# Phi loaded into the place of its transposed softmax, and the softmax's step ahead of the last mixing step

## The chip, the cores and the metric

The kernel runs on one core of a Trainium2 chip. The metric is the device time of one execution in microseconds (us), the median of several runs. The core has TensorE (PE in the profile; PEld is its weight load), VectorE (DVE), ScalarE (ACT), GpSimd (POOL) and SyncE (SP), whose queue issues the DMAs.

## The reference

For each of 8 batches and 8 heads with 576 tokens, head dimension 64 and 32 memory slots:

```python
a = exp(phi - max(phi, axis=2)); a = a / (sum(a, axis=2) + 1e-9)   # over the 576 tokens
k_m = einsum('bhsm,bhsd->bhmd', a, k)
v_m = einsum('bhsm,bhsd->bhmd', a, v)
attn = softmax(q @ k_m.T / 8)                                      # over the 32 slots
x = (attn @ v_m)  reshaped to [8, 576, 512]
u = x + real(fft(fft(x, axis=1), axis=2))
un = (u - mean(u)) / sqrt(var(u) + 1e-6)
out = u + relu(un @ w_ch1) @ w_ch2                                 # 512 -> 2048 -> 512
```

## The kernel before

There are two strands of work. **The feed-forward part (FFN)** runs over 18 chunks of 256 tokens. A chunk has 8 weight slices; for each slice `ffn1` makes 24 matmuls of 256 columns into `ph`, ScalarE and VectorE split the result into two 16-bit parts in `hring`, and `ffn2` makes 12 matmuls of 512 columns into `po`. Matmuls in 16 bits come in threes (high by high, high by low, low by high).

**The background** is a generator that makes the tokens `u` that the FFN takes, one batch after the other; a batch gives 4.5 tiles of 128 tokens, 2.25 chunks. Its steps for a batch are:

- the softmax of Phi over the tokens (`pooling_weights`): Phi (four DMAs of 160 KB, one for each pair of heads, `load_phi`) is transposed in 20 matmuls into three PSUM banks (`pl` and two `pf`, of a pool of four called `psg`), VectorE takes maxima (L398, L403), ScalarE the exponentials (L409, L410) into `pht`, VectorE the sums and reciprocals; then for each half ScalarE and VectorE write the high and the low part into `elt` (L418, L419), and a DMA transpose writes them into `et` (L301);
- for four pairs of heads: load the pair's k, v and q (`load_pair`; even pairs into `rawt`, odd pairs into `stg[:, 0]`, 640 KB for k and v and 384 KB for q), squares on ScalarE (L526, L529) that one matmul sums over the partitions (`pm<-scratch,small`), scaling and splitting (L541 to L547), the products with `et` (`pm<-et,stg`), and one step later the scores (`psc`) and their softmax. The transposed scores go into `stacks` by DMA transposes; stacks 0 and 1 lie in `attnT`, stacks 2 and 3 in `phs`;
- `values` (the transform of v_m over features, `pv`, and a DMA transpose into `vbdt`), `spectrum` (the transform over tokens, `pa` into `at`);
- three mixing steps: `mix_m` (`pp_t`), `mix_x` (`px_t`, which reads the stacks) and `add_mix` (L835) write `u` into a ring of 8 tiles. A mixing step waits in the program until the ring has room.

Between two `yield`s lies one step. After each weight slice but a chunk's last the loop takes at most one step, and at a chunk's end as many as the chunk after next needs. Batches 0 and 1 are special: they run at the start beside the loading of the weights, and batch 1's softmax is made apart by `next_weights`.

Before the change `phs` is the place of Phi, its first part `pht` the place of the exponentials, and its whole later that of stacks 2 and 3. `et` has 2560 16-bit elements for each partition, as many bytes as `phs`. In batches 2 to 7 the softmax is the batch's first step, and its loads stand at its head:

```python
        if b:
            load_phi(b)
        pl = psg.tile([P, 512], F32, tag="g", name=f"pl_{b}")
```

The order of each engine's queue and of SP's DMAs isn't the program's: a scheduler that works the timeline out ahead fixes it at build time, with the program's order as priority, so that a load can stand far ahead of its step when its place is free. Each engine then runs its own queue strictly in order.

Of the kernel before, what the change touches and what calls it, by code (L numbers as in the profile page):

```python
# [10 lines left out]
F32 = mybir.dt.float32  # L11
# [10 lines left out]
B, H, S, D, M = 8, 8, 576, 64, 32  # L22
NG = H // 2
# [5 lines left out]
NST = 5  # L29
KV = NST * 2 * P  # L30
KVP = KV + NST * 2 * M
# [10 lines left out]
NX = 2  # L42
# [95 lines left out]
def kernel(  # L138
# [10 lines left out]
    nc = tc.nc  # L149
# [11 lines left out]
    phs = const.tile([P, NST, NG, 2 * M], F32, name="phs")  # L161
    pht = phs.rearrange("p t g c -> p (t g c)")[:, : 2 * S].rearrange("p (g s) -> p g s", g=2)
    elt = const.tile([P, 2, NST * P], F16, name="elt")
    et = const.tile([P, 2, 2, NST, P], F16, name="et")
# [21 lines left out]
    identf = const.tile([P, P], F32, name="identf")  # L186
# [6 lines left out]
    stg = const.tile([P, 3, 4 * UW], F16, name="stg")  # L193
# [15 lines left out]
    def of_kind(t, w):  # L209
        return t[:, :, 1:3] if w else t[:, :, 0::3]  # L210

    qs = [stg[:, 2, 2 * nk + i * NQ : 2 * nk + (i + 1) * NQ] for i in range(2)]
    et32 = et.rearrange("p g l t c -> p (g l t c)").bitcast(F32).rearrange("p (g t c) -> p g t c", g=2, t=NST)


# [36 lines left out]
    def tiny(tag, n, bufs=2):  # L252
        if tag not in rings:
            rings[tag] = [taken[0], 0]
            taken[0] += n * bufs
        o, i = rings[tag]
        rings[tag][1] += 1
        o += i % bufs * n
        assert taken[0] <= 464, taken
        return scratch[:, o : o + n]  # L260
# [62 lines left out]


    def load_phi(b):
        for g in range(NG):
            nc.sync.dma_start(out=phs[:, :, g], in_=raw[b, g, :, KV:KVP].rearrange("p (t c) -> p t c", t=NST))

    def load_pair(b, g):
        r = rawt  # L330
# [53 lines left out]

    def pooling_weights(b):

        if b:
            load_phi(b)
        pl = psg.tile([P, 512], F32, tag="g", name=f"pl_{b}")
        mx = tiny("mx", 4, 2)  # L390
        pf = []
        for g in range(2):
            pf.append(psg.tile([P, 512], F32, tag="g", name=f"pf_{b}_{g}"))
            for t in range(NST):
                dst = pf[g][:, t * P : (t + 1) * P] if t < 4 else pl[:, g * P : (g + 1) * P]
                marks["pe"] = nc.tensor.transpose(dst, phs[:, t, 2 * g : 2 * g + 2].rearrange("p g c -> p (g c)"), identf)
            if b >= NX:
                nc.vector.tensor_reduce(out=mx[:, g : g + 1], in_=pf[g], axis=AX.X, op=ALU.max)  # L398
        rest = pl[:, : 2 * P].rearrange("p (g s) -> p g s", g=2)[:, :, : S - 4 * P]
        if b < NX:  # L400
            pooling_f32(b, pl, pf, rest)
            return
        nc.vector.tensor_reduce(out=mx[:, 2:4], in_=rest, axis=AX.X, op=ALU.max)  # L403
        nc.vector.tensor_tensor(out=mx[:, 0:2], in0=mx[:, 0:2], in1=mx[:, 2:4], op=ALU.max)
        nc.vector.tensor_scalar(out=mx[:, 0:2], in0=mx[:, 0:2], scalar1=-1.0, scalar2=None, op0=ALU.mult)
        su = tiny("su", 4, 2)
        for g in range(2):
            m = mx[:, g : g + 1]
            nc.scalar.activation(pht[:, g, : 4 * P], pf[g], AF.Exp, bias=m, accum_out=su[:, g : g + 1])  # L409
            nc.scalar.activation(pht[:, g, 4 * P :], rest[:, g], AF.Exp, bias=m, accum_out=su[:, 2 + g : 3 + g])  # L410
        nc.vector.tensor_tensor(out=su[:, 0:2], in0=su[:, 0:2], in1=su[:, 2:4], op=ALU.add)
        nc.vector.tensor_scalar(
            out=su[:, 0:2], in0=su[:, 0:2], scalar1=1e-9, scalar2=2.0**-EB, op0=ALU.add, op1=ALU.mult
        )
        nc.vector.reciprocal(out=su[:, 2:4], in_=su[:, 0:2])
        for g in range(2):
            r = su[:, 2 + g : 3 + g]
            nc.scalar.activation(elt[:, 0, :S], pht[:, g], AF.Copy, scale=r)  # L418
            nc.vector.scalar_tensor_tensor(  # L419
                out=elt[:, 1, :S], in0=pht[:, g], scalar=r, in1=elt[:, 0, :S], op0=ALU.mult, op1=ALU.subtract  # L420
            )
            transpose(
                et[:, g].rearrange("p l t c -> p (l t) c"), elt.rearrange("p l c -> p (l c)"), False, f"et_{b}_{g}"
            )
# [241 lines left out]
    def pair_transpose(b, g, ahl, attnT):  # L666
        if b:
            transpose(stacks[g], ahl.rearrange("p t k m -> p (t k m)"), False, f"attnT_{b}_{g}")
        else:
            transpose(attnT[:, g], ahl.rearrange("p t c -> p (t c)"), True, f"attnT_{b}_{g}")  # L670
# [497 lines left out]
    marks = {}  # L1168
# [6 lines left out]
    def background():  # L1175

        nt = 0
        u2, half_made = None, None
        for b in range(B):
            n = f"{b}"  # L1180
            ivs = tiny("ivs", NG)
            mem, ahl = {}, {}
            if b != 1:
                pooling_weights(b)
            yield (nt if half_made is None else half_made), 0
            if b == 0:

                for g in range(NG + 1):
                    if g < NG:
                        km = memory_f32(b, g, first[g], vmf, [0])  # L1190
                        mem[g] = first[g][:, KV:], None, km, 1.0 / 8.0
                    if g > 0:
                        ahl[g - 1] = pair_scores(b, g - 1, *mem.pop(g - 1), aeo)
                for g in range(NG):
                    memory_f32(b, g, first[g], vmf, [1])
            for step in range(NG + 2) if b > 0 else ():
                if step < NG:
                    r = load_pair(b, step)
                if step >= 2:
                    pair_transpose(b, step - 2, ahl.pop(step - 2), attnT)  # L1200
                if 0 <= step - 1 < NG:
                    ahl[step - 1] = pair_scores(b, step - 1, *mem.pop(step - 1), aeo)
                    yield (nt if half_made is None else half_made), 0
                if step < NG:
                    mem[step] = pair_memory(b, step, r, vmf, ivs)
                    yield (nt if half_made is None else half_made), 0
            vbd, vh, isg, igx, isq = values(b, vmf, ivs, ahl)
            yield (nt if half_made is None else half_made), 0
            at = spectrum(b, aeo)
            if b == 0:  # L1210
                transpose(vbdt, vbd, True, f"vbd_{b}")
                vbd = vbdt.rearrange("p (l g) f -> p l g f", l=2)
            for g in sorted(ahl):
                pair_transpose(b, g, ahl.pop(g), attnT)
            full = slice(0, P)
            for t in (0, 1, 2) if b % 2 == 0 else (2, 0, 1):
                yield (nt if half_made is None else half_made), 2 if t < 2 else 1 - b % 2
                if t == 2:
                    if b % 2 == 0:
                        u2 = uring[:, len(allocs) % NU]  # L1220
                        us[nt] = u2
                        allocs.append(nt)
                        half_made = nt
                        nt += 1
                    rows = slice(64 * (b % 2), 64 * (b % 2) + 64)
                    tm = mix_m(b, "t2", slice(256, 320), rows, at, vh, isg, isq)
                    px = mix_x(b, "t2", 4 * P + 64, 64, rows, attnT, vbd)
                    add_mix(u2, rows, px, igx, tm, 0)
                    half_made = nt - 1 if b % 2 == 0 else None
                    continue  # L1230
                tm = mix_m(b, f"t{t}", slice(t * P, (t + 1) * P), full, at, vh, isg, isg)
                for sign in range(2):
                    c0 = (2 * t + sign) * P
                    px = mix_x(b, f"t{t}{sign}", c0, P, full, attnT, vbd)
                    u = uring[:, len(allocs) % NU]
                    allocs.append(nt)
                    add_mix(u, full, px, igx, tm, sign)
                    us[nt] = u
                    nt += 1
            yield (nt if half_made is None else half_made), 0  # L1240
        while True:
            yield n_tiles, 0

    load_phi(0)
    marks["q"] = nc.sync.dma_start(out=mk, in_=mk_d)
    for g in range(NG):
        with tc.issue_after(marks["q"].ins):
            marks["q"] = nc.sync.dma_start(
                out=phi_next[:, :, g], in_=raw[1, g, :, KV:KVP].rearrange("p (t c) -> p t c", t=NST)
# [37 lines left out]
    for j in range(3):  # L1287
        load_weights(j)

    bg = background()  # L1290
    made, room = 0, 0

# [61 lines left out]
    for n in range(NW, n_steps):  # L1354
        c, j = divmod(n, NW)
# [97 lines left out]
```

## Time and profile before

| | |
|---|---|
| runs shown | 921.36, 923.54, 942.75 us; median 923.54 us |
| profiled execution | 920.78 us, its span 919.0 us |
| TensorE busy | 907.8 us, 99% of the span |
| VectorE, ScalarE, GpSimd busy | 622.3, 493.4, 266.6 us |
| granted TensorE clock | 1.0 |
| DMA queues | 100.16 MB, mean 109 GB/s |

The span runs from the first to the last instruction of the profiled execution; the time includes what lies around it. An engine's idle time is laid to what ended it. Matmuls are pipelined: the time of one (272 ns for 256 columns) is longer than the step from one to the next.

### The profile page before, as it was taken

Reading aid. Unit: us, or ns where it says so; the run is one execution under the profiler, and the core shown is the slowest. Engines: PE = TensorE matmul, PEld = TensorE weight load, DVE = VectorE, ACT = ScalarE, POOL = GpSimd, SP = SyncE. Lnnn points to the kernel's source line nnn. Section 1 sums busy time; section 2 is a strip of 40 time slices with the busy share of each in tenths; the row PEclk is TensorE's granted clock in tenths of the full one; section 3 lists DMA queues with packets and bytes.
Section 4 is the critical chain, followed back from the end, with each engine's and each line's share of the span. In section 5 each row is a group of like instructions: output and inputs, shape, how many; then the busy total and the mean of one; then the engine's idle time right before and its main releaser. Section 6 shows DMA issues by size and latency. Waiting matters only on the chain.

```text
span 919.0 us, 19338 instructions
## 1 busy us (share of the span) xinstructions
PE 907.8 (99%) x7796; PEld 671.4 (73%) x7796; DVE 622.3 (68%) x1471; ACT 493.4 (54%) x955; POOL 266.6 (29%) x302
## 2 busy tenths in 40 slices
PE   9999899999999999999999999999999999999998
PEld 8976567667766766776766667777676767688887
DVE  5979967667578775787554876676666776554554
ACT  4658867645464654664444564665555554533331
POOL 1304524224145231463143441152222231300000
PEclk9999999999999999999999999999999999999999
DMA  9938842433436352545224433365235353210000
GB/s 323 414 146 287 212 90 53 98 84 83 82 76 165 78 125 55 144 84 147 42 69 113 119 80 110 53 138 127 67 77 111 88 149 103 47 47 1 24 14 34
DMA packets 132761, 100.16 MB, mean 109 GB/s; under 512 B 115008, under 2 KB 115264, under 8 KB 130624
## 3 DMA queue, kind: packets, MB, share of 16 engines
q1 hardware_dynamic: 132672, 98.93, 40.9%
q8 instruction: 61, 1.00, 0.5%
q14 instruction: 28, 0.23, 0.1%
HBM read 62.35 MB, written 13.63 MB: 83 GB/s over the span
## 4 chain that ended last, share of the span: by engine, by line
PE 83%; DVE 7%; ACT 4%; issue 2%; DMA 2%; POOL 1%; SPq 0%; POOLq 0%; DVEq 0%; ACTq 0%
PE ph L318 34%; PE po L949 28%; PE po L1011 6%; PE pm L318 2%; PE pp_t L318 2%; PE psc L318 2%; PE po L910 1%; PE pa L748 1%; DMA et<-elt 1%; PE ph L893 1%; PE px_t L318 1%; PE pm L497 1%; DVE w2s L1100 1%; POOL ud L880 1%; PE idle L296 1%
## 5 line engine op out<-in xcount | busy, mean ns | idle before, releaser
L318 PE MATMUL ph<-unring,w1t 128*128 128x256 f16 x3264 | 389.0, 272 | 0.0
L318 PEld LDWEIGHTS <-w1t 128*128 128x128 f16 x3264 | 314.2, 98 | 58.8 <-issue 3.1
L949 PE MATMUL po<-w2s,hring 128*128 128x512 f16 x1344 | 310.1, 379 | 0.0
L949 PEld LDWEIGHTS <-hring 128*128 128x128 f16 x1344 | 130.0, 98 | 132.2
L940 DVE SCALAR_TENSOR_TENSOR hring<-ph,hring 128x512 f16<-128x512 f32 x112 | 76.0, 680 | 28.0 <-ACT hring L939 26.5
L939 ACT ACTIVATE hring<-ph 128x512 f16<-128x512 f32 x112 | 65.8, 589 | 52.0 <-PE ph L318 52.0
L859 POOL TENSOR_TENSOR scratch<-scratch,small 128x1 f32<-128x1 f32 x36 | 24.2, 674 | 180.1 <-DVE scratch L858 154.1
L634 POOL TENSOR_TENSOR aring<-aring,scratch 128x384 f32<-128x384 f32 x28 | 25.4, 908 | 165.5 <-DVE scratch L632 159.7
L880 POOL TENSOR_TENSOR ud<-un,ud 128x1024 f16<-128x1024 f32 x17 | 37.1, 2184 | 34.1 <-ACT ud L879 34.1
L318 PEld LDWEIGHTS <-stg 128*128 128x128 f16 x912 | 35.4, 97 | 6.3 <-issue 2.9
L658 ACT CAST aeo<-eo 128x384 f16<-128x384 f32 x30 | 15.3, 511 | 41.6 <-DVE eo L655 41.6
L628 ACT ACTIVATE aring<-aring,scratch 128x384 f32<-128x384 f32 x24 | 14.6, 610 | 42.4 <-DVE aring L627 42.3
L835 DVE SCALAR_TENSOR_TENSOR uring<-px_t,scratch,share 128x256 f32<-128x256 f32 (+1 forms) x80 | 34.2, 476 | 1.4 <-PE px_t L318 1.4
L646 ACT CAST at<-aring 128x640 f16<-128x640 f32 x28 | 20.3, 724 | 26.3 <-POOL aring L634 26.3
L618 DVE TENSOR_REDUCE scratch<-psc 128x12 f32<-128x384 f32 x32 | 17.5, 548 | 24.6 <-PE pm L318 18.9
L910 PE MATMUL po<-w2s,hring 128*128 128x512 f32 x64 | 31.2, 609 | 2.0 <-ACT hring L896 2.0
L1033 POOL TENSOR_TENSOR uring<-uring,share 128x256 f32<-128x256 f32 x3 | 2.2, 728 | 105.9 <-ACT share L1030 105.9
L821 DVE SCALAR_TENSOR_TENSOR share<-pp_t,scratch,small 128x257 f32<-128x257 f32 (+1 forms) x48 | 21.0, 480 | 15.5 <-ACT small L818 15.3
L651 DVE TENSOR_TENSOR eo<-aring 128x128 f32<-128x128 f32 x29 | 25.7, 885 | 8.5 <-POOL aring L649 8.5
L893 PE MATMUL ph<-unring,w1t 128*128 128x256 f32 x128 | 30.6, 383 | 0.0
L649 POOL TENSOR_TENSOR aring<-aring 128x128 f32<-128x128 f32 x56 | 30.0, 557 | 1.8
L893 PEld LDWEIGHTS ph<-unring,w1t 128*128 128x128 f32 x128 | 23.8, 190 | 7.7 <-issue 5.0
(320 smaller groups left out, 1546.3 us busy)
## 6 DMA issues: line engine op xcount, KB each, us to landing
out<-uring SPq DMA_DIRECT2D x35, 256.0 KB, 2.1
rawt<-in_raw SPq DMA_DIRECT2D x13, 640.0 KB, 5.2
stg<-in_raw SPq DMA_DIRECT2D x13, 640.0 KB, 5.3
stg<-in_w SPq DMA_DIRECT2D x7, 1024.0 KB, 6.8
rawt<-in_raw SPq DMA_DIRECT2D x15, 384.0 KB, 3.2
stg<-in_raw SPq DMA_DIRECT2D x15, 384.0 KB, 3.2
phs<-in_raw SPq DMA_DIRECT2D x28, 160.0 KB, 3.2
w2s<-in_w SPq DMA_DIRECT2D x4, 1024.0 KB, 11.0
```

Of the source, the lines that this page charges most:

```text
L318: m = nc.tensor.matmul(out, lhsT=lhsT, rhs=rhs, start=start, stop=stop)
L634: eng.tensor_tensor(out=a, in0=a, in1=sm.unsqueeze(2).to_broadcast([P, 12, M]), op=ALU.mult)
L649: eng.tensor_tensor(out=a2[:, i : i + 4], in0=a[:, 0:4], in1=a[:, 4:8], op=op)
L651: nc.vector.tensor_tensor(out=eo[:, 1:3, 0], in0=ap[:, 1:3, 0], in1=ap[:, 1:3, 1], op=ALU.add)
L835: nc.vector.scalar_tensor_tensor(out=u[rows, hs], in0=px[rows, hs], scalar=igx[rows], in1=tm[rows, w * NJ + half : w * NJ + half + 256], o ...
L880: marks[f"ul{c}"] = nc.gpsimd.tensor_tensor(out=ud[:, 1], in0=un, in1=ud[:, 0], op=ALU.subtract)
L893: nc.tensor.matmul(ph, lhsT=w[:, k, f * P : (f + 1) * P], rhs=unTs[0][:, k], start=(k == 0), stop=(k == NK - 1))
L910: nc.tensor.matmul(po[t], lhsT=h[:, f, t], rhs=w[:, f], start=(j == 0 and f == 0), stop=(j == NW - 1 and f == UB - 1),)
L939: marks["fa"] = nc.scalar.activation(h[:, 0], phv, AF.Relu)
L940: marks["fd"] = nc.vector.scalar_tensor_tensor(out=h[:, 1], in0=phv, scalar=0.0, in1=h[:, 0], op0=ALU.max, op1=ALU.subtract)
L949: nc.tensor.matmul(po[t], lhsT=hs[j][:, lh, f * 2 + t], rhs=w2s[:, j * UB + f, lw, :], start=(j == 0 and f == 0 and i == 0), stop=(j == NW ...
L1011: m = nc.tensor.matmul(po[n], lhsT=h[:, la, a], rhs=b[lb], start=(j == 0 and i == 0 and n in ("p1", "p6", "p5", "p4")), stop=(j == NW - 1 ...
```

## The change

Three things are done. Phi of batches 2 to 7 is loaded into the bytes of `et` (`phi_own`), where the transposed softmax will lie, and not into `phs`; the load stands after `values` of the batch before. The exponentials go into the first 1152 32-bit elements of `stg[:, 0]` (`pht_own`), where the odd pairs' k and v lie, and not into `phs`. And the softmax's step of batches 3 to 7 stands ahead of the last mixing step of the batch before, that of batch 2 at batch 1's end, where it was.

```diff
+    pht_own = stg[:, 0].bitcast(F32)[:, : 2 * S].rearrange("p (g s) -> p g s", g=2)
+    phi_own = et.rearrange("p g l t c -> p (g l t c)").bitcast(F32).rearrange("p (t g c) -> p t g c", t=NST, g=NG)
...
     def load_phi(b):
+        dst = phi_own if b else phs
         for g in range(NG):
-            nc.sync.dma_start(out=phs[:, :, g], in_=raw[b, g, :, KV:KVP].rearrange("p (t c) -> p t c", t=NST))
+            nc.sync.dma_start(out=dst[:, :, g], in_=raw[b, g, :, KV:KVP].rearrange("p (t c) -> p t c", t=NST))
...
     def pooling_weights(b):
-        if b:
-            load_phi(b)
+        phi, pht = (phi_own, pht_own) if b else (phs, None)
...
-                marks["pe"] = nc.tensor.transpose(dst, phs[:, t, 2 * g : 2 * g + 2].rearrange("p g c -> p (g c)"), identf)
+                marks["pe"] = nc.tensor.transpose(dst, phi[:, t, 2 * g : 2 * g + 2].rearrange("p g c -> p (g c)"), identf)
...
-            if b != 1:
+            if b == 0:
                 pooling_weights(b)
-            yield (nt if half_made is None else half_made), 0
+            if b < NX:
+                yield (nt if half_made is None else half_made), 0
...
             vbd, vh, isg, igx, isq = values(b, vmf, ivs, ahl)
+            if 0 < b < B - 1:
+                load_phi(b + 1)
             yield (nt if half_made is None else half_made), 0
...
-            for t in (0, 1, 2) if b % 2 == 0 else (2, 0, 1):
+            for i, t in enumerate((0, 1, 2) if b % 2 == 0 else (2, 0, 1)):
+                if i == 2 and 1 < b < B - 1:
+                    yield (nt if half_made is None else half_made), 0
+                    pooling_weights(b + 1)
                 yield (nt if half_made is None else half_made), 2 if t < 2 else 1 - b % 2
...
+            if b == 1:
+                yield (nt if half_made is None else half_made), 0
+                pooling_weights(2)
             yield (nt if half_made is None else half_made), 0
```

`NX` is 2.

## Rows read from the trace of the kernel before

**Rows 1.** The page: busy time of the engines, and the granted clock in 40 slices.
```profile
PE 907.8 (99%) x7796; PEld 671.4 (73%) x7796; DVE 622.3 (68%) x1471; ACT 493.4 (54%) x955; POOL 266.6 (29%) x302
...
PEclk9999999999999999999999999999999999999999
```

**Rows 2.** The chain of waits in order of time: start us, us, what.
```profile
175.06 4.08 DMA et<-elt
...
204.25 2.59 PE po L949 x12
...
241.17 2.62 PE ph L318 x24
...
278.00 3.41 DMA et<-elt
...
377.87 3.40 DMA et<-elt
```

**Rows 3.** The waits of TensorE: us in total, times, longest.
```profile
PE pm L318 <- DMA et<-elt: 2.2, 2, 1.9
...
PE pv L721 <- ACT share L702: 1.7, 1, 1.7
```

**Rows 4.** Windows: length, then busy us (instructions) of each engine; clock, DMA, GB/s.
```profile
92.00:140.00 48.00, 44.12 (x294) 30.78 (x293) 38.86 (x99) 35.19 (x65) 18.86 (x22) 1.00 0.60 145
...
240.00:285.00 45.00, 43.06 (x366) 30.32 (x365) 29.61 (x68) 23.59 (x51) 17.16 (x16) 1.00 0.39 87
...
780.00:919.00 139.00, 135.67 (x1185) 114.50 (x1181) 70.98 (x176) 47.11 (x72) 11.34 (x10) 1.00 0.11 28
```

**Rows 5.** Timeline of batch 3's softmax: start us, us, instruction, idle before it.
```profile
258.16 2.10 SPq L327 DMA_DIRECT2D phs<-in_raw  x4
...
265.07 0.60 PE L396 MATMUL pf<-identf,phs 128*128 128x128 f32 x4
...
270.32 0.21 ACT L410 ACTIVATION_READ_ACCUMULATOR phs<-pl,scratch 128x1 f32 x1
...
281.55 0.69 PE L318 MATMUL pm<-et,stg 128*128 128x64 f16 x20 [1.94 <-DMA et<-elt]
...
282.18 0.72 ACT L526 ACTIVATE stg<-stg 128x640 bf16<-128x640 f32 x1
282.31 0.82 DVE L419 SCALAR_TENSOR_TENSOR elt<-phs,scratch,elt 128x576 f16<-128x576 f32 x1 [1.81 <-ACT elt L418]
...
283.62 0.83 ACT L529 ACTIVATE stg<-stg 128x768 bf16<-128x768 f32 x1
```

**Rows 6.** Timeline of batch 3's pair 1: the matmul that sums its squares.
```profile
288.01 0.17 PE L318 MATMUL pm<-scratch,small 128*128 128x3 bf16 x1
```

**Rows 7.** Timelines of batch 2's softmax and its pairs 0 and 1.
```profile
152.71 3.15 SPq L327 DMA_DIRECT2D phs<-in_raw  x4
...
161.24 0.49 PE L396 MATMUL pf<-identf,phs 128*128 128x128 f32 x3
...
179.19 0.69 PE L318 MATMUL pm<-et,stg 128*128 128x64 f16 x20 [0.27 <-DMA et<-elt]
...
180.04 0.82 DVE L419 SCALAR_TENSOR_TENSOR elt<-phs,scratch,elt 128x576 f16<-128x576 f32 x1 [4.19 <-ACT elt L418]
...
185.80 0.17 PE L318 MATMUL pm<-scratch,small 128*128 128x3 bf16 x1
```

**Rows 8.** DMA issues by target and source: count, KB each, median us to landing.
```profile
stg<-in_raw SPq DMA_DIRECT2D x13, 640.0 KB, 5.3
...
phs<-in_raw SPq DMA_DIRECT2D x28, 160.0 KB, 3.2
```

**Rows 9.** The waits of SP's own queue: us in total, times, longest.
```profile
SPq L327 <- PE px_t L318: 52.8, 6, 13.7
```

**Rows 10.** Timeline of SP: loads of pair 1 for batches 2 and 3.
```profile
31.67 0.33 SPq L339 DMA_DIRECT2D stg<-in_raw  x1
...
225.76 2.42 SPq L339 DMA_DIRECT2D stg<-in_raw  x2
```

## The prediction, made before the change was run

> **What bounds the kernel now.** I read the page first. TensorE is busy for 99% of the span at full granted clock throughout, VectorE for 68%, ScalarE for 54% [rows 1]. A busy share alone doesn't prove a bound, so I looked at the pace of matmuls next: in the chain of waits, 24 ffn1 matmuls of 256 columns take 2.62 us (109 ns each) and 12 ffn2 matmuls of 512 columns take 2.59 us (216 ns each), and these two rows repeat with the same figures from 180 us to 890 us [rows 2]. That is one column per cycle at 2.4 GHz with nothing between. So where TensorE shows no gap, it issues at its pace, and only its gaps can be won.
>
> Then its gaps. TensorE's waits [rows 3] hold 2.2 us for the transposed softmax `et`: 1.94 us in batch 3 [rows 5] and 0.27 us in batch 2 [rows 7]; after 130 us no other line of TensorE stands in that list. The windows say the same from the other side: 240 to 285 us has 43.06 of 45.00 us busy, which is the gap of batch 3. What is left lies outside the change's reach or at its edge: 3.9 us idle between 92 and 140 us, of which 1.7 us wait for `share` in batch 1's values, and 3.3 us after 780 us, when all eight batches are mixed [rows 3, 4].
>
> **Part 1, Phi into `et`.** Removed: the four phi loads' wait for the last mixing step, because `phs` also holds stacks 2 and 3. The load's issue waits on SP for `px_t` 52.8 us in six batches [rows 9]; that is a queue's wait, not TensorE's. In batch 3 the loads are issued at 258.16 us, right after the last mixing matmuls, and the first transpose of Phi starts at 265.07 us: 6.9 us [rows 5]; in batch 2 it is 152.71 to 161.24 us: 8.5 us [rows 7]. Landing takes 3.2 us of it [rows 8]; the rest is issue, and a TensorE queue that has other work first. The new loads need only that the batch before has used `et` in its four memory products, tens of us earlier. The bytes are the same, four times 160 KB [rows 8]. The moved issues pass other work on SP, at 2.1 us for four [rows 5]; the DMA that follows them there (the transpose of vbd or an output) has slack, so I cost this at nothing; without that slack it would be 2.1 us in each of six batches, 12.6 us, if all of it came through to TensorE.
>
> **Part 2, exponentials into the raw odd pairs' place.** The exponentials and the two scalings by batch are the same instructions with another address: 0. But pair 1's k and v of the same batch lie there too. Today they are loaded a whole batch ahead: the pair that batch 3 uses at 282.18 us was issued at 225.76 us, and batch 2's already at 31.67 us [rows 5, 10]. After the change this load cannot start before the second `elt` difference has read the exponentials. In batch 3 that ends at 282.31 + 0.82 = 283.13 us [rows 5]. Now the new chain: 5.3 us to landing [rows 8] gives 288.4 us; the three squares run from 282.18 to 283.62 + 0.83 = 284.45 us today [rows 5], 2.3 us, so they would end at 290.7 us. TensorE's one matmul that sums their results stands at 288.01 us [rows 6]. **At the old place of the softmax the new wait would cost 2.7 us**; batch 2 gives the same: 180.86 + 5.3 + 2.3 = 188.5 against 185.80 us [rows 7], 2.7 us. Behind that matmul on TensorE stand ffn1 and ffn2, since its queue is in order, so this would be lost in full. It is covered if the softmax ends at least 2.7 us earlier.
>
> **Part 3, the softmax's step in front of the last mixing step.** I walked through the counters that decide which step is taken with which weight slice. Batch 2's softmax keeps its slot; batches 3 and 7 swap it with the last mixing step and so get it one slot earlier, while pair 0 stays; batches 4, 5 and 6 get the softmax, and pair 0 too, at least one slot earlier (batch 5's softmax a whole chunk). No chunk's normalisation moves. A slot holds 2.62 + 2.59 = 5.2 us of FFN on TensorE [rows 2]. So in batches 3 to 7 the softmax moves forward by about 6.9 us of phi wait and 5.2 us of slot, against 2.7 us needed; in batch 2 by up to 8.5 us. The new load is hidden, and the `et` waits go: -2.2 us. What is late next is nothing that TensorE shows.
>
> The cost that stays unknown is in TensorE's queue order: it is worked out ahead, instruction by instruction, and one wrong guess of a DMA's time gave the 1.94 us gap of batch 3 [rows 5]. The new load of 640 KB is one more such guess in six batches. Lower end: none, and the phi guess that goes instead is worth up to the 2.2 us; upper end: 2.7 us in each batch. I take 0, nearest to the rows in which pair loads today hide, and keep both ends.
>
> A rule that speaks for more: the Trainium skill, "Perfetto Trace Analysis", section "Identifying the Most-Contended Engine", says that matmul busy time is no good measure of how near TensorE is to its limit and names the weight loads' busy share instead. That is 73% here and would leave 27% of the span, some 248 us, as room. The rows disagree: twelve 512-column matmuls fill 2.59 us without a gap [rows 2] and need only one load apiece, so the load path idles while the columns run at full pace.
>
> **The sum** against the profiled execution: 920.78 us (its span is 919.0 us, 1.8 us lies around it) - 2.2 = 918.5 us. The three runs shown have a median of 923.54 and a lowest of 921.36 us, so usual runs stand 0.6 to 2.8 us above the profiled one, the middle 1.7: 918.5 + 1.7 = 920.2. I forecast **920 us**.
>
> **Rivals.**
> (a) *The new wait takes over.* Pair 1's load behind the exponentials comes late to the sum's matmul: 2.7 us in each of six batches, 16 us: 936 us. It decides from the point where a batch's softmax ends less than 2.7 us earlier than now relative to pair 1. Against it: 6.9 us of phi wait gone. For it: in batch 2 nothing else helps, since its softmax keeps its slot. Batch 2 alone gives 923 us; four batches give 931 us.
> (b) *PSUM banks; slower.* The softmax holds three of the four banks of its pool from the first transpose to the last exponential, 265.07 to 270.53 us, 5.5 us [rows 5]. Now the last mixing step, which needs two banks, comes behind it in five batches. If its matmuls stand in TensorE's queue with no FFN between, it costs 5.5 us in each: 27 us, 947 us, 2.6% slower than the median. It decides where less than 5.5 us of FFN lies between; a slot holds 5.2 us, which leaves 0.3 us a batch, and in batches 4, 5 and 6 the mixing waits for the chunk's end anyway.
> (c) *Gain at the start.* Phi of batch 2 no longer waits, so its 20 transposes (0.11 us apart, 2.2 us) and what follows may fill part of the 3.9 us idle before 140 us [rows 4]: 920 - 3.9 = 916 us at best, and 920.78 - 2.2 - 3.9 = 914.7 us if the runs come as low as the profiled one.
> (d) *It does nothing.* The `et` wait in batch 3 comes from the order, not from Phi's arrival, and comes back elsewhere: 922.5 us.
> (e) *TensorE has room.* The chain holds 4.08, 3.41 and 3.40 us of `et` transpose for batches 2, 3 and 4 [rows 2]; if such pieces were time that TensorE could win, 10.9 us came out in place of 2.2: 911.5 us. Against it stands that TensorE shows only 2.2 us of waits in these places [rows 3]. The section of the Trainium skill cited above would lead here.
>
> **How the numbers follow.** The forecast, with anything from -3 to +2 us about it, 0.60; (a) in one to all batches 0.17; (b) 0.05; (c) 0.08; (d) 0.07; (e) 0.03. Two per cent, 18.5 us, is about what a measurement here tells from no change: faster means below 905 us, slower above 942 us. Faster holds only what goes beyond (e), 0.01. Slower holds most of (b) and a doubled (a), where the issue on SP adds its 2.1 us in each batch, 0.05. The rest, 0.94, is within. The range 914 to 932 us takes in (c), (d), and (a) up to four batches with the 0.6 us by which runs scatter; outside stay (a) in all batches, (b) and (e).
>
> **What would show it.** Right: no TensorE wait for `et` in the waits; the phi loads' issue 10 us and more ahead of the transposes in every batch, with no SP wait for `px_t` at that line; pair 1's k and v issued after the second `elt` difference, and the squares of pair 1 still over before the sum's matmul; TensorE full between 140 and 780 us. Wrong: a gap in front of the sum's matmul or pair 1's products (a), a gap in front of `px_t` or `pp_t` with the exponentials as releaser (b), a changed idle sum before 140 us (c). A TensorE that stays full while the time moves by more than 5 us would mean that its pace, not its gaps, had changed, and that I misread the bound.

## The result and the profile after

The changed kernel takes 926.53 us (median of six runs, 925.53 to 945.31), the kernel before 921.65 us in the same session (median of six); the ratio is 1.0055 with a 95% interval of 1.0041 to 1.0068. Forecast was 920 us and a small gain. Runs of both kernels near 943 us show a lower mean clock (0.978 in the changed kernel's) and are left out of every ratio and of the table's medians, and the profile of experiment 10 below is of such a run. The profiled execution took 926.56 us with a span of 924.8 us: 5.8 us more than before.

The page, busy time of the engines (compare [rows 1]): the same 7796 instructions on TensorE, 2.1 us more busy, and 3.7 us more idle.

```profile
PE 909.9 (98%) x7796; PEld 670.1 (72%) x7796; DVE 624.2 (67%) x1471; ACT 493.1 (53%) x955; POOL 267.8 (29%) x302
```

TensorE's waits from 130 us on: total us, times, longest (compare [rows 3]). Both `et` waits are gone. In their place stand five others, 6.2 us in place of 2.2 when added up from the timelines: 4.0 us more.

```profile
PE pm L320 <- ACT stg L528: 2.7, 1, 2.7
PE psc L320 <- DVE scratch L589: 1.6, 1, 1.6
PE psc L320 <- ACT scratch L588: 0.9, 1, 0.9
PE pm L320 <- POOL stg L546: 0.7, 1, 0.7
PE pm L320 <- ACT stg L543: 0.2, 1, 0.2
```

Windows of the same kernel (length, busy us of each engine, then granted clock, DMA share, GB/s). The first three follow the largest wait; the last three answer to [rows 4].

```profile
178.00:183.50 5.50, 2.89 (x40) 2.55 (x38) 1.85 (x7) 1.84 (x7) 0.00 (x0) 1.00 0.73 179
183.50:187.00 3.50, 3.38 (x10) 1.34 (x10) 2.86 (x11) 2.62 (x5) 0.00 (x0) 0.51 0.02 5
187.00:193.00 6.00, 6.00 (x46) 3.95 (x44) 5.18 (x8) 3.37 (x6) 4.84 (x6) 1.00 0.38 95
...
92.00:140.00 48.00, 44.39 (x300) 31.32 (x300) 38.93 (x101) 35.69 (x67) 19.67 (x22) 1.00 0.58 144
240.00:285.00 45.00, 44.27 (x397) 31.61 (x395) 29.43 (x70) 24.27 (x52) 15.78 (x15) 1.00 0.41 100
780.00:925.00 145.00, 141.45 (x1246) 118.87 (x1242) 75.90 (x189) 49.57 (x78) 11.88 (x11) 1.00 0.10 27
```

Right behind the wait the granted clock stands at half (0.51, the 1.2 GHz level) for 3.4 us, which costs 1.7 us. Twelve ffn2 matmuls take 4.30 us there (timeline of batch 2 below); counted the same way they take 2.75 us at full clock, in a timeline of the kernel before:

```profile
187.35 2.75 PE L949 MATMUL po<-w2s,hring 128*128 128x512 f16 x12
```

With 4.0 us of waits that is 5.7 of the 5.8 us. The half clock does not come in every run: two of the changed kernel's runs have a mean clock of 1.000 and take 925.53 and 925.79 us, the profiled one and another 0.998 and 926.5 us, one 0.996 and 928.4 us. It is slower without it too.

**Batch 2**, timeline of the kernel after: start us, us, instruction, idle before it (compare [rows 7, 10]).

```profile
159.09 0.60 PE L398 MATMUL pf<-identf,et 128*128 128x128 f32 x4
...
176.85 0.82 DVE L421 SCALAR_TENSOR_TENSOR elt<-stg,scratch,elt 128x576 f16<-128x576 f32 x1 [3.73 <-ACT elt L420]
...
177.69 0.33 SPq L342 DMA_DIRECT2D stg<-in_raw  x1
...
182.02 0.74 ACT L528 ACTIVATE stg<-stg 128x640 bf16<-128x640 f32 x1 [3.02 <-DMA stg<-in_raw]
...
183.38 0.19 ACT L528 ACTIVATION_READ_ACCUMULATOR stg<-stg 128x1 f32 x1
183.62 0.17 PE L320 MATMUL pm<-scratch,small 128*128 128x3 bf16 x1 [2.73 <-ACT stg L528]
183.81 4.30 PE L951 MATMUL po<-w2s,hring 128*128 128x512 f16 x12
```

Read it from the bottom. TensorE's sum matmul waits for ScalarE's squares, these for pair 1's k and v, and the load that brings them is issued 0.02 us after the second `elt` difference has ended at 177.67 us; before, it was issued at 31.67 us [rows 10]. Phi itself is early: its loads go out at 35.70 us, in the timeline of SP in the kernel after, where they went out at 152.71 us [rows 7].

```profile
35.70 13.16 SPq L330 DMA_DIRECT2D et<-in_raw  x4
```

Still the first Phi transpose comes only 2.15 us earlier than before (159.09 for 161.24 us), and the second `elt` difference 3.2 us (177.67 for 180.86 us). TensorE has no wait in front of these transposes; the order in which it takes its queue sets this, not Phi.

**Batch 4**, timeline of the kernel after: score steps of VectorE beside instructions of GpSimd, and the two waits of `psc`.

```profile
395.09 2.13 POOL L882 TENSOR_TENSOR ud<-un,ud 128x1024 f16<-128x1024 f32 x1
395.16 2.13 DVE L654 SCALAR_TENSOR_TENSOR eo<-aring,small 128x64 f32<-128x64 f32 x1 [0.40 <-POOL aring L636]
...
398.76 2.16 POOL L962 TENSOR_TENSOR un<-w2s 128x1024 f32<-128x1024 f16 x1
398.87 2.27 DVE L657 TENSOR_TENSOR eo<-aring 128x192 f32<-128x192 f32 x1
401.06 0.28 DVE L569 TENSOR_REDUCE scratch<-pm 128x64 f32<-128x128 f32 x1
...
402.13 0.22 PE L320 MATMUL psc<-scratch,stg 128*128 128x64 f16 x2 [0.91 <-ACT scratch L588]
...
403.33 0.74 DVE L589 TENSOR_TENSOR scratch<-scratch 128x64 f16<-128x64 f32 x1
404.12 0.64 PE L320 MATMUL psc<-scratch,stg 128*128 128x64 f16 x16 [1.63 <-DVE scratch L589]
```

One line's durations in the same kernel (min, median, max ns) show that 2.27 us is the longest of 29 equal instructions:

```profile
L657 DVE TENSOR_TENSOR eo<-aring x29: 343/348/2271, 26.2 to 769.3; 128x192 f32<-128x192 f32 x29
```

VectorE's L657, a subtraction of scores, runs as long as GpSimd's addition beside it (L962), both end within 0.3 us, and the normalisation behind it (L569, L588, L589), for which TensorE waits, is late. In the kernel before, the same GpSimd addition lay beside another line of VectorE, whose two instructions took 2.87 us together, and TensorE's next product started at 395.90 us without a wait:

```profile
393.36 2.87 DVE L547 SCALAR_TENSOR_TENSOR stg<-stg,scratch 128x320 f16<-128x320 f32 x2
393.49 2.38 POOL L960 TENSOR_TENSOR un<-w2s 128x1024 f32<-128x1024 f16 x1
...
395.90 0.31 PE L318 MATMUL pm<-et,stg 128*128 128x64 f16 x5
```

**Batch 3**, where the new load is hidden as foreseen (timeline after; compare [rows 5, 6]):

```profile
255.69 0.63 PE L398 MATMUL pf<-identf,et 128*128 128x128 f32 x4
...
272.75 1.33 DVE L421 SCALAR_TENSOR_TENSOR elt<-stg,scratch,elt 128x576 f16<-128x576 f32 x1 [2.10 <-ACT elt L420]
274.10 0.34 SPq L342 DMA_DIRECT2D stg<-in_raw  x1
...
281.00 0.18 ACT L531 ACTIVATION_READ_ACCUMULATOR stg<-stg 128x1 f32 x1
284.23 0.17 PE L320 MATMUL pm<-scratch,small 128*128 128x3 bf16 x1
```

The squares end at 281.2 us, 3.0 us ahead of the matmul that sums them.

### The profile page after: what moved, and what is told of

The parts are those of the page before. It is cut to its first block, busy times and chain, and to the rows that moved or that the text cites. A ratio compares the mean times of both kernels' runs of the same rounds, so it can differ in the third digit from the quotient of the medians.

```text
span 924.8 us, 19340 instructions
## 1 busy us (share of the span) xinstructions
PE 909.9 (98%) x7796; PEld 670.1 (72%) x7796; DVE 624.2 (67%) x1471; ACT 493.1 (53%) x955; POOL 267.8 (29%) x302
## 5 line engine op out<-in xcount | busy, mean ns | idle before, releaser
L882 POOL TENSOR_TENSOR ud<-un,ud 128x1024 f16<-128x1024 f32 x17 | 37.1, 2185 | 30.5 <-ACT ud L881 30.5
L661 POOL TENSOR_TENSOR aeo<-eo,aeo 128x256 f16<-128x256 f32 x30 | 23.4, 780 | 30.2 <-ACT aeo L660 30.1
```

Source lines behind the costliest of these rows:

```text
L882: marks[f"ul{c}"] = nc.gpsimd.tensor_tensor(out=ud[:, 1], in0=un, in1=ud[:, 0], op=ALU.subtract)
```

## The experiments

The theory after the two traces: the loss has two places. In batch 2, pair 1's load now stands behind the exponentials with too little ahead of it; in batch 4, the pair's step, taken earlier, puts VectorE's score steps beside GpSimd's addition. Rivals: Phi's early arrival alone upsets TensorE's queue; the step's new place alone costs the time, whatever lies in it; batch 4's waits come from the pair's new slot and not from GpSimd. Each table row has the median of the runs that the ratio counts and their number, the ratio to the kernel before with its interval, the span of the profiled execution (919.0 us before), and the sum of TensorE's listed waits after 130 us (2.2 us before).

| run | median us (n) | ratio | span | waits |
|---|---|---|---|---|
| after | 926.51 (5) | 1.0055 [1.0041, 1.0068] | 924.8 | 6.2 |
| 1 exponentials in `aeo` | 923.50 (6) | 1.0025 [1.0014, 1.0037] | 922.4 | 3.5 |
| 2 batch 2's in `phs` | 922.92 (9) | 1.0017 [1.0006, 1.0028] | 920.5 | 3.4 |
| 3 Phi into `et` alone | 921.55 (9) | 0.9999 [0.9989, 1.0009] | 919.7 | 2.8 |
| 4 step not moved | 935.21 (4) | 1.0148 [1.0130, 1.0166] | 931.2 | 13.0 |
| 5 pairs in old slots | 921.96 (10) | 1.0004 [0.9994, 1.0013] | 920.3 | 2.7 |
| 6 slice 2's sum short | 921.00 (10) | 0.9995 [0.9986, 1.0004] | 919.3 | 1.8 |
| 7 exponentials moved alone | 928.49 (3) | 1.0070 [1.0052, 1.0089] | 928.0 | 9.0 |
| 8 `aeo`, step not moved | 921.42 (10) | 1.0000 [0.9991, 1.0009] | 919.7 | 2.7 |
| 9 slice 3's sum short | 921.00 (9) | 0.9995 [0.9985, 1.0005] | 918.7 | 1.9 |
| 10 sums a chunk later | 922.89 (8) | 1.0015 [1.0005, 1.0025] | – | – |

**1, `e1_exp_in_aeo`.** Parts 1 and 3 stay; the exponentials go to a buffer that is free at that time, so pair 1's load doesn't wait for them.

```diff
-    pht_own = stg[:, 0].bitcast(F32)[:, : 2 * S].rearrange("p (g s) -> p g s", g=2)
+    pht_own = aeo.rearrange("p l t e h c -> p (l t e h c)").bitcast(F32)[:, : 2 * S].rearrange("p (g s) -> p g s", g=2)
```

> The changed kernel, but the exponentials go into the place of the even and odd score sums (aeo), which is free between a batch's spectrum and the next batch's first scores, so no pair's load waits for them. Theory A (the cost is pair 1's load queued behind the exponentials, in batch 2 above all, 2.7 us of wait and about 1.7 us of half clock after it): TensorE's wait for the squares in batch 2 is gone, 919 to 923 us. Theory B (the step's new place costs, by a worse order of TensorE's queue): 925 us or more. Theory C (Phi's early loads disturb the loading of the weights): 925 us or more.

Pair 1's load is early again and the wait for the squares is gone, in SP's timeline and TensorE's waits of this kernel:

```profile
35.62 0.33 SPq L342 DMA_DIRECT2D stg<-in_raw  x1
```
```profile
PE psc L320 <- DVE scratch L589: 1.6, 1, 1.6
PE psc L320 <- ACT scratch L588: 0.9, 1, 0.9
PE pm L320 <- POOL stg L546: 0.7, 1, 0.7
PE pm L320 <- ACT stg L543: 0.3, 1, 0.3
```

The ratio falls by 0.0030, 2.8 us, which is the 2.73 us wait. The median of 923.5 us lies just above theory A's 919 to 923 us and below the 925 us of the others. Batch 4's two waits stay as they were, so they are a second cause; and the profiled execution has its half clock behind these now (mean 0.76 from 397 to 404 us).

**2, `e2_batch2_exp_in_phs`.** Like the changed kernel, but batch 2 alone keeps its exponentials in `phs`.

```diff
-        phi, pht = (phi_own, pht_own) if b else (phs, None)
+        phi, pht = (phi_own, <view of phs> if b == 2 else pht_own) if b else (phs, None)
```

> The changed kernel, but batch 2 alone has its exponentials in the old place, so that its pair 1 is loaded far ahead again; batches 3 to 7 are as changed. Theory A: the 2.7 us wait in batch 2 and the half clock after it are gone, about 922 us; what is left over the kernel before is some 2 us of waits for the score products in batch 4. Theories B and C: 925 to 927 us, since only one batch's buffer differs.

One batch's place takes the whole wait away, as the timeline of this kernel shows for the sum's matmul in batch 2; in batches 3 to 7 the load behind the exponentials costs no wait that shows.

```profile
182.84 0.17 PE L320 MATMUL pm<-scratch,small 128*128 128x3 bf16 x1
```

The same 0.91 and 1.63 us waits in batch 4 bring no half clock in the profiled execution (mean 1.000 from 397 to 404 us), whose span is 1.9 us below experiment 1's. That is a difference between executions and not between the kernels: of experiment 2's nine runs counted, four have a mean clock of 0.998, of experiment 1's six three.

**3, `e3_phi_only`.** The kernel before with part 1 alone.

```diff
+        dst = phi_own if b else phs
...
-        if b:
-            load_phi(b)
+        phi = phi_own if b else phs
...
+            if 0 < b < B - 1:
+                load_phi(b + 1)
```

> The kernel before with the first part alone: Phi of batches 2 to 7 loaded into et after the values of the batch before; exponentials in the old place, the step at its batch's head. Theory A: no new wait, the wait for et in batch 3 gone or smaller, 919 to 922 us. Theory C: 924 us or more, with the loss before 60 us. Theory B: 919 to 922 us.

No change in time. Its waits of TensorE:

```profile
PE pm L319 <- DMA et<-elt: 1.8, 2, 1.0
PE psc L319 <- ACT scratch L587: 1.0, 1, 1.0
```

Batch 3's wait for `et` of 1.94 us became 0.76 us, one of 0.98 us in front of `psc` came after it in the same batch, and one of 1.04 us for `et` in batch 4. Phi's early arrival neither wins nor loses: the rival that puts the loss on it falls, and so does the thought that it frees the `et` waits.

**4, `e4_step_not_moved`.** The changed kernel without part 3: the softmax's step at the head of its batch again.

```diff
-            if b == 0:
+            if b != 1:
                 pooling_weights(b)
-            if b < NX:
-                yield (nt if half_made is None else half_made), 0
+            yield (nt if half_made is None else half_made), 0
...
-                if i == 2 and 1 < b < B - 1:
-                    yield (nt if half_made is None else half_made), 0
-                    pooling_weights(b + 1)
...
-            if b == 1:
-                yield (nt if half_made is None else half_made), 0
-                pooling_weights(2)
```

> The changed kernel without its third part: Phi in et, exponentials in the odd pairs' place, the step at its batch's head. Theory A: the wait in batch 2 stays (its step has not moved in the changed kernel either), and pair 1's load may come late in other batches too: 926 to 936 us. Theory B: the loss goes with the move, 921 to 923 us.

8.6 us slower than the changed kernel, so part 3 is what keeps the loss small. The largest of its waits of TensorE:

```profile
PE pm L320 <- ACT stg L528: 4.5, 2, 2.9
PE po L951 <- DVE uring L1058: 2.4, 1, 2.4
PE psc L320 <- ACT scratch L588: 1.7, 1, 1.7
```

The squares are late in batch 2 (2.87 us) and batch 6 (1.60 us), and the seven other lines of the list hold 8.5 us, where all waits of the kernel before are 2.2 us. Behind the 2.87 us the clock stays full (mean 1.000 from 180 to 190 us).

**8, `e8_aeo_step_not_moved`.** Experiment 4 with the exponentials in `aeo`, by the same line as in experiment 1.

> Phi in et, the exponentials in aeo, the step at its batch's head; against the run that differs in the exponentials' place alone (935 us). Theory A: all of that run's loss is pair 1's load behind the exponentials, so 920 to 923 us. Rival: a good part of it is another cost of the unmoved step with Phi in et, 928 us or more.

Back to 1.0000. All of experiment 4's 13.8 us (935.21 less 921.42; each beside the same kernel before at 921.55 and 921.23) is the load behind the exponentials. Without that load in the way the step's old place stands at 1.0000 and its new one, experiment 1, at 1.0025. The waits for `et` are still there (0.76 and 0.94 us), as in experiment 3; they go only where the step is moved.

**7, `e7_exponentials_moved_alone`.** The kernel before with part 2 alone.

```diff
+    pht_own = stg[:, 0].bitcast(F32)[:, : 2 * S].rearrange("p (g s) -> p g s", g=2)
...
+        pht = pht_own if b else None
```

> The kernel before with the second part alone: the exponentials in the odd pairs' place, Phi in phs and the step at its batch's head. Theory A: pair 1's k and v start only after the second elt difference, some 2.7 us late for the sum of squares in up to six batches: 930 to 938 us. Theory B and C: 921 to 923 us.

A loss of 6.5 us by the ratio and 7.3 us by the medians (928.49 for 921.23 us), a little under theory A's range, with 3.8 us of waits for the squares in four batches; the two largest of TensorE's waits:

```profile
PE pm L319 <- ACT stg L528: 3.8, 4, 1.4
PE psc L319 <- ACT scratch L588: 2.0, 2, 1.2
```

That is less than half of the 16 us at which rival (a) priced six batches: no batch waits more than 1.4 us for its squares here, and batches 2 and 5 not at all. TensorE's order is worked out anew with the late load known, which may be the reason; no run tests it.

**5, `e5_pairs_in_old_slots`.** Experiment 1, but the pairs of batches 4 to 6 keep their slots; only the softmax moves.

```diff
-            if b < NX:
+            if b < NX or 3 < b < B - 1:
                 yield (nt if half_made is None else half_made), 0
```

> The run with the exponentials in aeo, and an empty step at the head of batches 4, 5 and 6, so that their pairs of heads keep the slots of the kernel before while the softmax stays ahead of the last mixing step. Theory A (the 2.5 us wait for batch 4's score products comes from the pairs being one slot earlier, where GpSimd's sums of the weights run beside VectorE's score sums): that wait is gone or under 1 us, 920 to 922 us. Theory B (it comes from the softmax standing ahead of the mixing step): the wait stays, 923 to 925 us.

1.0025 became 1.0004, and batch 4's waits 1.65 us in place of 2.54 us. So the pair's slot is part of it, but the waits did not go. In this kernel's timeline L657 is short again, and the same GpSimd addition lies beside L654 instead:

```profile
393.93 2.13 POOL L962 TENSOR_TENSOR un<-w2s 128x1024 f32<-128x1024 f16 x1
394.00 2.13 DVE L654 SCALAR_TENSOR_TENSOR eo<-aring,small 128x64 f32<-128x64 f32 x1 [0.40 <-POOL aring L636]
...
397.81 0.34 DVE L657 TENSOR_TENSOR eo<-aring 128x192 f32<-128x192 f32 x1
```

**6, `e6_short_gpsimd_sum`.** Experiment 1 with GpSimd's first addition of weight slice 2 on one column of each half, 2 in place of 1024; this leaves out most of that slice's weight sum.

```diff
+        if j == 2:
+            nc.gpsimd.tensor_tensor(out=t[:, :, 0:1], in0=w[:, :, 0, 0:1], in1=w[:, :, 1, 0:1], op=ALU.add)
+        else:
+            nc.gpsimd.tensor_tensor(out=t, in0=w[:, :, 0], in1=w[:, :, 1], op=ALU.add)
```

> The run with the exponentials in aeo, where GpSimd's first addition for the sums of weight slice 2 (in chunk 5, beside batch 4's pair 1) makes one column in each half and not 512; this leaves out part of the weight sums of that slice. Theory A: VectorE's score sum at that place takes 0.35 us and not 2.3 us, the wait for batch 4's score products falls below 1 us, 921 to 922.5 us. Theory B (TensorE's order alone makes the wait): the wait stays at 2.5 us, 924 us.

It missed the addition it was meant for: the shortened one lay at 374 us, and the two of the collision still ran together, at 393 us:

```profile
393.19 2.17 POOL L965 TENSOR_TENSOR un<-w2s 128x1024 f32<-128x1024 f16 x1
393.31 2.27 DVE L657 TENSOR_TENSOR eo<-aring 128x192 f32<-128x192 f32 x1
```

Yet batch 4's wait fell to 0.8 us. VectorE was ahead by then: it reached L657 1.6 us earlier than in experiment 1 (393.31 for 394.92 us), and at 375 us its L576 took 0.23 us here and 1.19 us beside the full addition there. So the collision cost TensorE only what VectorE had no lead for.

**9, `e9_short_gpsimd_sum_slice3`.** The same edit with `j == 3`, which is the addition of the collision; it leaves out most of slice 3's sum.

> As the run with GpSimd's short addition, but for slice 3, whose addition is the one that really lies beside batch 4's pair 1 (in the run before it the shortened one lay 20 us earlier); part of that slice's weight sums is left out. Theory A: VectorE's score sum beside it takes 0.35 us and not 2.27 us, and the 2.5 us wait for batch 4's score products is under 1 us: 921 to 922 us. Theory B (TensorE's order alone): the wait stays at 2.5 us though the score sum is short, 924 us.

```profile
394.43 0.24 POOL L963 TENSOR_TENSOR un<-w2s 128x2 f32<-128x2 f16 x1
394.53 0.35 DVE L657 TENSOR_TENSOR eo<-aring 128x192 f32<-128x192 f32 x1
...
398.04 0.64 PE L320 MATMUL psc<-scratch,stg 128*128 128x64 f16 x16 [0.96 <-DVE scratch L589]
```

VectorE's subtraction is back at 0.35 us, the waits fall from 2.54 to 0.96 us, and the ratio from 1.0025 to 0.9995. This shows that the collision makes 1.6 us of the waits; the rest of the ratio's 2.8 us fits the half clock, which three of experiment 1's six runs show (mean 0.998) and none of the nine here. What is left may be the other one, L654 beside L882, which still takes 2.13 us here; that was not tried.

**10, `e10_weight_sums_a_chunk_later`.** Experiment 1 with the constant that places the weight sums raised from 3 to 4.

```diff
-C1 = 3
+C1 = 4
```

> The run with the exponentials in aeo, all work kept, with GpSimd's sums of the weights one chunk later (chunks 4 to 11). Theory A: the wait for batch 4's score products moves or goes, since other work now lies beside GpSimd; the time stays between 920 and 925 us, as the same collisions come elsewhere. A wait of 2.5 us at the same place would speak for theory B.

A miss of design. The eight slices' sums follow one another, so the addition of the slice before now stands in the same place: GpSimd's at 414.16 us takes 2.17 us, VectorE's L657 at 414.27 us 2.27 us (this profile runs 19.4 us behind experiment 1's there), and both waits stand as in experiment 1. By its expectation that would speak for theory B, but the collision was there too, so it tells nothing apart.

## Why the prediction was wrong

**What held.** The bound: the time moved by what TensorE's gaps and its clock cost, 5.7 of 5.8 us, with the same instructions. The `et` waits went, SP's wait for `px_t` at the Phi load fell from 52.8 us [rows 9] to 3.2 us, and in batches 3 to 7 the new load is hidden: in batch 3 the second `elt` difference came 9.1 us earlier (274.08 for 283.13 us) and the sum's matmul only 3.8 us (284.23 for 288.01 us), 5.3 us of cover against the 2.7 us needed. No bank wait (b) shows, the idle time from 92 to 140 us only went from 3.9 to 3.6 us (c), and nothing of (e) came. Rival (d) missed the time, but its reason, that the `et` wait comes from the order and not from Phi's arrival, is what experiment 3 shows. The range held the time; the sign did not hold.

**The step that failed** is in part 3: "in batch 2 by up to 8.5 us. The new load is hidden". The 8.5 us from the load's issue to the first transpose were read as time that Phi's arrival costs. They were mostly time in which TensorE's queue had other work first, as part 1 itself said of "the rest": with Phi's loads all issued by 49 us the transpose moved by 2.15 us and the second difference by 3.2 us. And the other end moved more: without the wait the sum's matmul would have stood at 180.9 us, 4.9 us earlier than 185.80 us, because the order of the queue was made anew. So the slack between them shrank from 4.9 to 3.2 us, and the chain (4.35 us to the squares' start, 1.55 us of two squares; priced at 5.3 and 2.3 us) needs 5.9 us: 2.7 us are missing. Rival (a) gave batch 2 alone those 2.7 us and 923 us, and named the reason, that nothing else helps there; it had the size by luck, with two misses that cancel: a chain 1.7 us too long and a slack 1.7 us too large. Experiments 1 and 2 show this cause.

**What was priced at nothing.** "What is late next is nothing that TensorE shows": the pair's step in batches 4 to 6, moved a slot earlier, puts VectorE's L657 beside GpSimd's addition in batch 4, and 2.54 us of waits follow. Experiment 9 shows that the collision makes 1.6 us of them, experiment 5 the slot's part. Of the unknown cost of TensorE's order, 0 to 2.7 us a batch, 0 was taken; it came to this and 0.7 us for `stg` in batch 3 where the `et` wait had been.

Of the collision itself the rows show 0.35 us alone and 2.27 us beside GpSimd's 2.16 us. The Trainium skill, "SBUF — State Buffer", section "Who interferes with whom", says that a VectorE instruction with two inputs in SBUF contends with a GpSimd instruction that reads SBUF, since they share a pair of ports. The trace agrees: with GpSimd's addition cut to 0.24 us VectorE's took 0.35 us again.

**What was not in the sum at all** is the half clock, 1.7 us in the profiled execution. It isn't the change's alone: of the 21 runs of the kernel before counted beside experiments 1 to 4, eight have a mean clock of 0.998 and a median of 922.6 us, nine 1.000 and 921.2 us, so that the medians hold some of it on both sides. And the gain was too high from the start: "the `et` waits go: -2.2 us" took their end for a saving, but TensorE's order brings others. Experiment 3, with part 1 alone, has 2.8 us of waits, 1.8 of them for `et`; experiment 9, with no wait for `et` and none for the squares, still has 1.9 us and stands at 0.9995. Nothing tried beats the kernel before by more than its interval.

**Open:** why the half clock follows a wait in one execution and not in another of the same kernel; what batch 4's last 0.96 us are; why the load behind the exponentials costs 13.8 us with Phi in `et` (experiment 4) and about 7 without (experiment 7). Experiment 7's span grew by 9.0 us, its listed waits after 130 us by 6.8; the other 2.2 us are busy time of TensorE (910.0 for 907.8 us) at full clock. An estimate from [rows 2] and the 272 ns of one matmul: a wait also leaves bare the end of the matmul before it, 272 less 109 ns, and 11 more waits make 1.8 us of that.

## What to carry to other kernels

Before a buffer's place is given to something new, look when its next load is issued today: here a load that went out 146 us earlier (31.67 for 177.69 us) became the middle of a chain, and one batch of six without cover cost 2.7 us where the waits to be won were 2.2 us. Cover has two ends; a step comes earlier only if what held it was the thing removed, and the consumer's place in a queue that is planned anew moves as well. Try the same idea with a place that nothing is loaded into (experiments 1 and 8) before moving steps around it, and count what a moved step will lie beside on VectorE and GpSimd.

## What the runs showed of the hardware

In the profiled executions the granted clock fell to 1.2 GHz for 3.4 us after a wait of 2.73 us in the changed kernel, and after waits of 0.91 and 1.63 us in experiment 1; after the same 0.91 and 1.63 us in experiment 2 and after 2.87 us in experiment 4 it stayed at 2.4 GHz. So these gaps in TensorE cost their own length, and in some executions another 1.7 us; four of experiment 2's nine runs have a mean clock of 0.998 and take 923.7 to 924.0 us, the five at 1.000 take 922.0 to 922.9 us. A GpSimd instruction over 1024 columns stretched the two-input VectorE instructions that lay beside it in batch 4: 0.35 to 2.27 us (L657), 0.47 to 2.13 us (L654), 0.23 to 1.19 us (L576, which began 1.0 us after it).
